# Gated linear attention and a mixture of experts on one core: output matmuls by term, column sums in mid-step, another bank for one tile, and a new step plan at the start

## The chip, the cores and the metric

The kernel runs on one core of one Trainium2 chip. The metric is the device time of one execution in microseconds (us). Engines are named as in the profile: PE is TensorE's matmul, PEld its weight load, DVE is VectorE, ACT is ScalarE, POOL is GpSimd, SP is SyncE, which issues the DMAs.

## The reference

Attention first: for each of 4 batches and 8 heads a state of 48 by 48 decays by a gate and takes an outer product at each of 768 positions. Its outputs are the tokens (3072 by 384) of a mixture of 8 experts, whose weights are balanced over tokens and experts in eight rounds.

```
f = 1 / (1 + exp(-f_logit))
for t in range(S):
    state = f[:, :, t, :, None] * state + einsum('bhd,bhe->bhde', k[:, :, t], v[:, :, t])
    y[:, :, t] = einsum('bhd,bhde->bhe', q[:, :, t], state)
x = y as (3072, 384)
P = exp(x @ w_gate - max)
for _ in range(8):
    P /= P.sum(1, keepdims=True) + 1e-09
    P /= P.sum(0, keepdims=True) + 1e-09
    P *= N / E
out = sum over e of P[:, e:e+1] * (relu(x @ w1[e]) @ w2[e])
```

## The kernel before

Every fp32 matrix is split into two fp16 halves, high and low (xh and xl, w1h and w1l, hh and hl and so on), and a product takes three matmuls: high by high, low by high, high by low. The high half is made by ACT, the low one by DVE, from the same source, so a low half follows its high half.

The work is in three stages.

**Lead stage (to some 390 us).** 24 items, each 128 positions of one batch and all heads, in two chunks of 64, run through a chain of steps: gates by ACT's sigmoid, decay products by DVE's scans (`r`, and the one written over `fl`, which the profile calls q), scaled keys `kb` in two halves, their transposes `kt`, scores `aps`, masked scores `am` and their halves `ah`, `al`, new states `kvps`, `st` and their halves `sh`, `sl`, and the outputs `yps`. From `yps` ACT makes xh and DVE xl, the tokens; the matmul `lps` gives the gate logits. Items 0, 1 and 2 use `early_item` (transposes on PE), the others `item` (transposes by DMA). Each `yield` in an item ends a step. A loop counts steps in `g`: in each it advances every live item by one step, then the weight loads that are due in this step (`loads[g]`, set with `at_steps`), and then takes work from a filler:

```
        for gen in loads.pop(g, []):
            next(gen, None)
        put_off[0] = g < 18
        fill([n for at_, n in FILL if g >= at_][-1])
```

The filler is the first two experts on the tokens that are ready, tile by tile (`moe_tile`: 128 tokens; two groups of 36 matmuls `hps` of 128 columns, then 24 matmuls `yps<-w2,h` of 384 columns) for the first three of eight groups of tokens, and `moe` (384 tokens) for the others. `fill(n)` issues n units; a unit is one matmul of 384 columns or three of 128. `FILL` gives the units per step: (12, 4.7) means 4.7 units a step from step 12 on. A filler tile ends with `yr`, an ACT copy, and a DMA to a scratch buffer; its `hl` (lines 382 and 431) is DVE's low half of the hidden layer, which may be put off and made up for (`settle`). Regular items start every 8 steps from step 22 (`LEADS`), and their DMAs four steps earlier.

All instructions are pinned: each engine takes them in the order in which the program issues them, so a step's place in the program is its place in each engine's queue. SP is a queue too: a DMA that waits for its buffer holds those behind it.

Expert 0's weights are `first[0..7]` (four pieces of w1, four of w2), expert 1's `second[0..7]`. Each is a generator of three steps: DMA; then the high half on ACT (line 346); then the low half on DVE (line 350). Their raw pieces share buffers, so the second expert's DMA of a piece waits for the first's conversion.

`warm(n)` issues n matmuls on constants, whose result is not used; the first item begins with `warm(20)` while its data are on the way.

**Middle stage (to 502 us).** `sinkhorn` balances the weights in steps (its column sums are a matmul `sk_c` with a matrix of ones, lines 127 to 136), beside the rest of the filler, `fill(LEAD)` with LEAD = 8 in each step, and beside `convert` and `prepare_w1`, which make sums and halves for the last stage. The last three pairs of the filler are `raws`.

PSUM tiles of the filler come from two pools of two banks each in turn (`bank`: an even count takes `psm`, an odd one `psn`). At the end of the stage `psn` and the items' banks are given up to the pool `pk`.

**Last stage (to the end).** Experts 2 to 7 by a scheme with 15 products in place of 18 (banks kb_A to kb_F), and their second layer `kyps`. The change does not touch it.

In `item`, the outputs are issued for each of four head pairs p and two chunks c, six matmuls each, the fifth of them the first that reads `sl`:

```
                pr = [(vhw, ah[:, n, :]), (vlw, ah[:, n, :]), (vhw, al[:, n, :])]
                if c >= c0:
                    pr += [(shw[:, w], qh[:, cs[n]]), (slw[:, w], qh[:, cs[n]]), (shw[:, w], ql[:, cs[n]])]
```

`early_item` already issues them term by term. Line 278 is the helper `mm`, through which all matmuls of this path go.

Of the kernel before, what the change touches and what calls it, by code (L numbers as in the profile page):

```python
# [12 lines left out]
ALU = mybir.AluOpType  # L13
# [5 lines left out]
NP = H // 2  # L19
C = 64  # L20
# [56 lines left out]
NB = NP * CT  # L77
TS = CT * C
LEADS = 22
FILL = ((0, 12), (1, 10), (2, 0), (5, 2), (6, 0), (7, 6), (11, 0), (12, 4.7), (22, 8.7), (43, 8.2))  # L80
LEAD = 8
EPRIO = 100
WPRIO = 150
# [18 lines left out]
def sinkhorn(nc, pool, psp, tag, identf, onesf, lg, pe, mm, pin, scale=1.0):  # L102
    sm = pool.tile([128, 2], F32, name="sk_sm")
    pin(nc.vector.tensor_reduce(out=sm[:, 0:1], in_=lg.rearrange("p a e -> p (a e)"), axis=AX.X, op=ALU.max))
    yield
    ps = psp.tile([128, 128], F32, name="sk_t", tag=tag)
    mm(transpose=True, out=ps[0:1, :], in_=sm[:, 0:1], identity=identf)
    row = pool.tile([1, 1], F32, name="sk_r")
    yield
    pin(nc.vector.tensor_reduce(out=row, in_=ps[0:1, :], axis=AX.X, op=ALU.max))  # L110
    yield
    ps = psp.tile([128, 1], F32, name="sk_m", tag=tag)
    mm(out=ps, lhsT=onesf[0:1, :], rhs=row, start=True, stop=True)
    yield
    pin(nc.vector.tensor_scalar(out=sm[:, 1:2], in0=ps, scalar1=-scale, scalar2=None, op0=ALU.mult))
    pin(nc.scalar.activation(out=pe, in_=lg, func=AF.Exp, bias=sm[:, 1:2], scale=scale))
    yield
    yield
    rs = pool.tile([128, NT], F32, name="sk_rs")
    cs = pool.tile([128, NE], F32, name="sk_cs")  # L120
    for it in range(8):
        pin(nc.vector.tensor_reduce(out=rs, in_=pe, axis=AX.X, op=ALU.add))
        pin(nc.vector.tensor_scalar(out=rs, in0=rs, scalar1=1e-9, scalar2=None, op0=ALU.add))
        pin(nc.vector.reciprocal(out=rs, in_=rs))
        yield
        pin(nc.vector.tensor_tensor(out=pe, in0=pe, in1=rs[:, :, None].to_broadcast([128, NT, NE]), op=ALU.mult))
        pin(nc.vector.tensor_reduce(out=cs, in_=pe.rearrange("p a e -> p e a"), axis=AX.X, op=ALU.add))
        yield
        ps = psp.tile([128, NE], F32, name=f"sk_c{it}", tag=tag)
        mm(out=ps, lhsT=onesf, rhs=cs, start=True, stop=True)  # L130
        yield
        pin(nc.vector.tensor_scalar(out=cs, in0=ps, scalar1=1e-9, scalar2=None, op0=ALU.add))
        pin(nc.vector.reciprocal(out=cs, in_=cs))
        pin(nc.vector.tensor_scalar(out=cs, in0=cs, scalar1=float(N / NE), scalar2=None, op0=ALU.mult))
        yield
        pin(nc.vector.tensor_tensor(out=pe, in0=pe, in1=cs[:, None, :].to_broadcast([128, NT, NE]), op=ALU.mult))
        yield
# [3 lines left out]
def general(ctx, tc, qkf, vt, wg, w1, w2, out):  # L141
# [63 lines left out]
    lg = gc.tile([128, NT, NE], F32, name="glg")  # L205
    pe = gc.tile([128, NT, NE], F32, name="gpe")
    nc.sync.dma_start(out=lg.rearrange("p (u t) e -> p u t e", t=TT), in_=lgd.rearrange("u p t e -> p u t e"))
    for _ in sinkhorn(nc, gc, gs, "ps", identf, onesf, lg, pe, lambda transpose=False, **kw: (nc.tensor.transpose if transpose else nc.tensor.matmul)(**kw), lambda ins: ins):
        pass
    nc.sync.dma_start(out=ped.rearrange("u p t e -> p u t e"), in_=pe.rearrange("p (u t) e -> p u t e", t=TT))  # L210

    with tc.For_i(0, U) as u:
# [37 lines left out]
def fast(ctx, tc, qkf, vbd, wg, w1, w2, out, flag):  # L250
# [18 lines left out]
    def pin(ins):  # L269
        engine = ins.ins.engine  # L270
        if fixed[0]:
            if engine in last:
                behind(ins, last[engine])
            last[engine] = ins
        return ins

    def mm(transpose=False, **kw):
        ins = (nc.tensor.transpose if transpose else nc.tensor.matmul)(**kw)  # L278
        if order:
            behind(ins, order[-1])  # L280
        order.append(ins)
# [52 lines left out]
    def load(e, k, j):  # L334
        src = (w1 if k == 1 else w2)[e, j]
        n = 4 * (k - 1) + j
        if n < 6:
            raw = xp.tile([128, 1152], F32, name=f"w{k}r_{e}_{j}", tag=f"x{'hl'[n % 2]}{3 - n // 2}", bufs=1)[:, 0:768]
        else:
            raw = rp.tile([128, 768], F32, name=f"w{k}r_{e}_{j}", tag="wraw")  # L340
        raw = raw.rearrange("p (a f) -> p a f", f=256 if k == 1 else DM)
        nc.sync.dma_start(out=raw, in_=src)
        yield
        wh, wl = ((wp1 if e else wp0).tile(list(raw.shape), F16, name=f"w{k}{q}_{e}_{j}", tag=f"w{q}") for q in "hl")
        scale = W1S if k == 1 else W2S
        pin(nc.scalar.activation(out=wh, in_=raw, func=AF.Copy, scale=scale))
        pair = [wh, None]
        ws[e][k - 1].append(pair)
        yield
        pin(nc.vector.scalar_tensor_tensor(out=wl, in0=raw, scalar=scale, in1=wh, op0=ALU.mult, op1=ALU.subtract))  # L350
        pair[1] = wl
# [140 lines left out]
    def warm(n):  # L492
        ps = bank([128, 512], f"wps{banks[0]}")
        for _ in range(n):
            mm(out=ps, lhsT=ind[:, 0:128], rhs=ind[:, 0:NB * C], start=True, stop=True)

    def settle(n=2):
        for low in owed[:n]:
            low()
        del owed[:n]  # L500

    def early_item(i):
# [59 lines left out]
            pin(nc.vector.tensor_tensor(out=carry[0, i + 1], in0=kv1[0:R], in1=st[:, 1], op=ALU.add))  # L562

        if not i:
            warm(20)
        transposed(0, 0)
        yield
        for rs, ks in heads:
# [37 lines left out]
        c0 = 0 if i else 1  # L606
        pin(nc.scalar.activation(out=sh[:, c0:], in_=st[:, c0:], func=AF.Copy, scale=SS))
        settle()
        if i:
            transposed(0, 1)  # L610
            transposed(1, 1)
        yield
        pin(nc.vector.tensor_tensor(out=al, in0=am, in1=ah, op=ALU.subtract))
        pin(nc.vector.scalar_tensor_tensor(out=sl[:, c0:], in0=st[:, c0:], scalar=SS, in1=sh[:, c0:], op0=ALU.mult, op1=ALU.subtract))
        yield
        if not i:
            xt[0] = xalloc(0)
# [35 lines left out]
    def item(i):  # L653
# [93 lines left out]
        xh, xl = xof(u)  # L747
        tok = slice(s % TT * TS, s % TT * TS + TS)
        yps = psa.tile([128, NP, TS], F32, name=f"yps_{i}", tag="y", bufs=1)
        for p in range(NP):  # L750
            for c in range(CT):
                n, w = CT * p + c, slice((c * NP + p) * 96, (c * NP + p) * 96 + 128)
                vhw, vlw = vhs[i % 3][:, w], vls[i % 3][:, w]
                pr = [(vhw, ah[:, n, :]), (vlw, ah[:, n, :]), (vhw, al[:, n, :])]
                if c >= c0:
                    pr += [(shw[:, w], qh[:, cs[n]]), (slw[:, w], qh[:, cs[n]]), (shw[:, w], ql[:, cs[n]])]
                for m, (a, x) in enumerate(pr):
                    mm(out=yps[:, p, c * C:(c + 1) * C], lhsT=a, rhs=x, start=(m == 0), stop=(m == len(pr) - 1))
        yield
        for si, so in PCS:  # L760
            pin(nc.scalar.activation(out=xh[so + (tok,)], in_=yps[si], func=AF.Copy, scale=YS * XS))
# [121 lines left out]
    def go(gen, n=1):  # L883
        for _ in range(n):
            next(gen, None)

    first = [load(0, 1 + n // 4, n % 4) for n in range(8)]
    second = [load(1, 1 + n // 4, n % 4) for n in range(8)]
    wgen = gate_weights()
# [25 lines left out]
    for n in range(2, 8):  # L915
        at_steps(first[n], *((0,), (5,), (0, 7), (0, 8), (3, 9), (5, 10))[n - 2])
    for n in range(8):
        at_steps(second[n], 4 + n, *((17, 20), (17, 20), (18, 21), (18, 21), (22, 25), (23, 26), (24, 27), (25, 28))[n])
    begin = {LEADS + STEPS * (i - 3): i for i in range(3, NT)}
    while live or g < max(begin):  # L920
        if g == 2:
            third = early_item(2)
            go(third)
        if g == 7:
            go(third)
        if g == 10:
            live.append(third)
        if g + 4 in begin:
            live.append(item(begin[g + 4]))
        for it in list(live):  # L930
            if next(it, it) is it:
                live.remove(it)
        for gen in loads.pop(g, []):
            next(gen, None)
        put_off[0] = g < 18
        fill([n for at_, n in FILL if g >= at_][-1])
        g += 1
    actx.close()
    xq = ctx.enter_context(tc.tile_pool(name="xq", bufs=1, reuse_waits="tile"))
# [100 lines left out]

    def raws():
        for e, u in RAW[-3:]:
            yield from moe(e, u, ws[e])
            done[0] += 1

# [8 lines left out]
    converts = [convert(b, left(b)) for b in range(B)]  # L1054
    work = [converts[0]]
    kw = None
    step = 0
    while True:
        more = fill(LEAD)
        if not more and kw is None:  # L1060
            wctx0.close()
            kw = ctx.enter_context(tc.tile_pool(name="kw", bufs=4, reuse_waits="tile"))
            filler = raws()
            more = fill(0)
        if not more:
            break
        next(chain, None)
        for gen in list(work):
            if next(gen, work) is work:
                work.remove(gen)  # L1070
        step += 1
        if step in (28, 50, 66):
            work.append(converts[{28: 1, 50: 2, 66: 3}[step]])
        if step == 46:
            work.append(chained(prepare_w1(ORDER[0][0], j) for j in range(2)))
    for _ in chain:
        pass
    for gen in work:
        if gen is not converts[3]:
            for _ in gen:  # L1080
# [223 lines left out]
```

## Time and profile before

| | |
|---|---|
| median of 3 runs | 1555.04 us (1554.15 to 1555.78) |
| the profiled execution | 1555.37 us, span 1553.6 us |
| granted clock of PE, mean | 0.997 |
| PE busy | 1522.1 us (98%), 13462 matmuls |
| DVE, ACT, POOL busy | 1097.2, 776.5, 514.5 us |

A row of a timeline has start (us from the span's start), time, engine, line, operation, what it writes and reads, size and count, and in brackets the idle time of the engine just before it and what ended it. Rows of busy time by stretch have the stretch, its length, then busy us of PE, PEld, DVE, ACT and POOL with instruction counts, then the granted PE clock, the share of the DMA engines and GB/s. A matmul's own time holds its latency; matmuls overlap, so their cost is the distance between starts.

### The profile page before, as it was taken

To read this page: it belongs to the slowest core of one execution; us is meant where nothing else is said; L and a number is where in the kernel's file an instruction comes from. 1 tells how busy PE (TensorE), PEld (TensorE's weight loads), DVE (VectorE), ACT (ScalarE), POOL (GpSimd) and SP (SyncE) were. 2 spreads that over 40 slices of the span, in tenths; PEclk is the share of its full clock that TensorE was granted. 3 is DMA by queue.
4 is the path that set the end of the run, shared out by engine and by line. 5 is a ranking of instruction groups with operands and counts; after the bars stand their busy time and mean duration, and the time that the engine had idled before them with its cause. 6 is when DMAs were issued, how large, how long until landed. Compare 5 with 4: busy or idle time off the path is not lost.

```text
span 1553.6 us, 32490 instructions
## 1 busy us (share of the span) xinstructions
PE 1522.1 (98%) x13462; PEld 1105.9 (71%) x13462; DVE 1097.2 (71%) x1810; ACT 776.5 (50%) x1489; POOL 514.5 (33%) x656
## 2 busy tenths in 40 slices
PE   7899999999999999999999999999999999999998
PEld 5688886666555777777777777777777777777775
DVE  8887888885775766676767776666766666665654
ACT  6655565553343655555455554545444444445432
POOL 1244444444519102333333322223222232222211
PEclk9999999999999999999999999999999999999999
DMA  9355554441002122232322231121112112000011
GB/s 267 102 137 132 127 140 120 119 116 31 26 22 63 55 72 79 63 89 67 92 67 82 77 87 62 41 62 51 62 47 66 44 38 57 22 20 12 6 57 65
DMA packets 89679, 114.39 MB, mean 74 GB/s; under 512 B 50641, under 2 KB 67153, under 8 KB 89521
## 3 DMA queue, kind: packets, MB, share of 16 engines
q1 hardware_dynamic: 89520, 112.22, 25.7%
q8 instruction: 107, 1.75, 0.5%
q14 instruction: 52, 0.42, 0.1%
HBM read 88.41 MB, written 14.16 MB: 66 GB/s over the span
## 4 chain that ended last, share of the span: by engine, by line
PE 90%; DVE 6%; ACT 1%; POOL 1%; issue 1%; ACTq 0%; DVEq 0%; POOLq 0%
PE kyps L278 36%; PE yps L278 12%; PE hps L278 9%; PE kb_A L278 8%; PE kb_B L278 8%; PE kb_D L278 6%; PE kb_C L278 4%; PE kb_E L278 2%; PE kb_F L278 2%; PE kvps L278 1%; PE aps L278 1%; POOL xs L962 1%; PE wps L278 1%; DVE hl L382 1%; DVE w2l L350 0%
## 5 line engine op out<-in xcount | busy, mean ns | idle before, releaser
L1119 POOL TENSOR_TENSOR acc<-acc,yt 128x384 f32<-128x384 f32 x172 | 173.3, 1007 | 629.8 <-ACT yt L1118 629.8
L278 PE MATMUL kyps<-k2l,kh 128*128 128x384 f16 x1152 | 375.5, 326 | 0.0
L278 PE MATMUL kyps<-k2h,kl 128*128 128x384 f16 x1152 | 375.5, 326 | 0.0
L278 PE MATMUL kyps<-k2h,kh 128*128 128x384 f16 x1152 | 375.5, 326 | 0.0
L278 PEld LDWEIGHTS <-k1h 128*128 128x128 f16 x2880 | 281.5, 98 | 70.4
L278 PEld LDWEIGHTS <-kh 128*128 128x128 f16 x2304 | 225.4, 98 | 103.9
L1118 ACT ACTIVATE yt<-kyps,pes 128x384 f32<-128x384 f32 x172 | 100.0, 581 | 323.1 <-PE kyps L278 321.2
L278 PEld LDWEIGHTS <-k1l 128*128 128x128 f16 x1440 | 140.6, 98 | 64.1 <-issue 7.1
L1115 DVE SCALAR_TENSOR_TENSOR acc<-kyps,pes,acc 128x384 f32<-128x384 f32 x92 | 56.9, 618 | 172.0 <-PE kyps L278 172.0
L278 PEld LDWEIGHTS <-kl 128*128 128x128 f16 x1152 | 112.7, 98 | 44.7
L1212 ACT ACTIVATE cp<-kb_A 128x512 f32<-128x512 f32 x144 | 86.2, 598 | 86.3 <-PE kb_A L278 85.8
L278 PE MATMUL yps<-w2h,hl 128*128 128x384 f16 x384 | 125.6, 327 | 3.5 <-DVE hl L431 3.5
L278 PE MATMUL yps<-w2l,hh 128*128 128x384 f16 x384 | 125.5, 327 | 1.8 <-DVE w2l L350 1.8
L278 PE MATMUL yps<-w2h,hh 128*128 128x384 f16 x384 | 125.5, 327 | 0.2 <-DVE hl L382 0.2
L278 PEld LDWEIGHTS <-w1h 128*128 128x128 f16 x1344 | 97.4, 98 | 35.4 <-issue 4.6
L1212 ACT ACTIVATE cp<-kb_B 128x512 f32<-128x512 f32 x144 | 87.1, 605 | 49.9 <-DVE kb_B L1214 49.8
L278 PEld LDWEIGHTS <-hh 128*128 128x128 f16 x768 | 74.6, 98 | 47.5 <-issue 2.8
L1217 DVE TENSOR_TENSOR cp<-kb_D,cp 128x512 f32<-128x512 f32 x144 | 98.8, 686 | 12.8 <-PE kb_D L278 11.8
L278 PE MATMUL hps<-xl,w1h 128*128 128x128 f16 (+1 forms) x672 | 84.9, 257 | 1.4 <-DVE xl L640 0.7
L278 PE MATMUL hps<-xh,w1h 128*128 128x128 f16 (+1 forms) x672 | 84.1, 257 | 1.7 <-ACT xh L637 1.1
L278 PE MATMUL hps<-xh,w1l 128*128 128x128 f16 (+1 forms) x672 | 84.4, 258 | 0.0
L278 PE MATMUL kb_A<-xbh,k1h 128*128 128x256 f16 x288 | 78.5, 273 | 0.8 <-ACT yr L399 0.6
(244 smaller groups left out, 3616.9 us busy)
## 6 DMA issues: line engine op xcount, KB each, us to landing
wm<-in_w_dram SPq DMA_DIRECT2D x64, 384.0 KB, 3.0
q<-in_qkf_dram SPq DMA_DIRECT2D x23, 672.0 KB, 5.2
vr<-in_vbd_dram SPq DMA_DIRECT2D x24, 384.0 KB, 3.5
ys<-yr SPq DMA_DIRECT2D x48, 192.0 KB, 2.4
k1r<-in_w_dram SPq DMA_DIRECT2D x24, 384.0 KB, 3.0
k2r<-in_w_dram SPq DMA_DIRECT2D x24, 384.0 KB, 3.0
yb<-ys SPq DMA_DIRECT2D x48, 192.0 KB, 2.3
out_dram<-acc SPq DMA_DIRECT2D x24, 192.0 KB, 1.9
```

Of the source, the lines that this page charges most:

```text
L278: ins = (nc.tensor.transpose if transpose else nc.tensor.matmul)(**kw)
L382: held[0] = pin(nc.vector.scalar_tensor_tensor(out=tl, in0=ps, scalar=0.0, in1=th, op0=ALU.max, op1=ALU.subtract))
L962: pin(nc.gpsimd.tensor_tensor(out=block(r), in0=block(p), in1=block(q), op=ALU.add if op == '+' else ALU.subtract))
L1115: pin(nc.vector.scalar_tensor_tensor(out=y, in0=ps, scalar=p, in1=y, op0=ALU.mult, op1=ALU.add))
L1118: pin(nc.scalar.activation(out=yt, in_=ps, func=AF.Copy, scale=p))
L1119: pin(nc.gpsimd.tensor_tensor(out=y, in0=y, in1=yt, op=ALU.add))
L1212: pin(nc.scalar.activation(out=fresh(ev[2]), in_=bk, func=AF.Copy))
L1217: pin(nc.vector.tensor_tensor(out=fresh(ev[4]), in0=bk, in1=old, op=ALU.add if ev[2] == '+' else ALU.subtract))
```

## The change

Six edits.

1. `warm(20)` before the first item's transposes becomes `warm(12)`.
2. In `early_item`, for items 1 and 2, the two transposes of the second chunk are issued one step later, behind `al` and `sl`. Item 2 takes its second and third step at steps 6 and 9 in place of 7 and 10, and all that follow one sooner; its DMAs stay at step 2. The units per step are cut anew: none at step 9, six at 10 and 11, 5.3 from 12, 8.7 from 21, 8.1 from 43. Low parts of the filler are put off until step 17, not 18.
3. The second expert's halves are made one to three steps sooner, its DMAs are issued where they were; from step 21 on the due loads stand behind the step's filler, not ahead of it.
4. In `item`, the outputs are issued term by term over all p and c, with the terms that read `sl` last.
5. In `sinkhorn` the column sum's matmul is handed to the loop, which issues it after 5 of the next 8 units.
6. Ahead of the last pair of the filler the bank count skips one where that puts the last tile into `psm`.

```
-FILL = ((0, 12), (1, 10), (2, 0), (5, 2), (6, 0), (7, 6), (11, 0), (12, 4.7), (22, 8.7), (43, 8.2))
+FILL = ((0, 12), (1, 10), (2, 0), (5, 2), (6, 0), (7, 6), (9, 0), (10, 6), (12, 5.3), (21, 8.7), (43, 8.1))
...
-        mm(out=ps, lhsT=onesf, rhs=cs, start=True, stop=True)
-        yield
+        yield lambda: mm(out=ps, lhsT=onesf, rhs=cs, start=True, stop=True)
...
-            warm(20)
+            warm(12)
...
         settle()
+        yield
+        pin(nc.vector.tensor_tensor(out=al, in0=am, in1=ah, op=ALU.subtract))
+        pin(nc.vector.scalar_tensor_tensor(out=sl[:, c0:], in0=st[:, c0:], scalar=SS, in1=sh[:, c0:], op0=ALU.mult, op1=ALU.subtract))
         if i:
             transposed(0, 1)
             transposed(1, 1)
-        yield
-        pin(nc.vector.tensor_tensor(out=al, in0=am, in1=ah, op=ALU.subtract))
-        pin(nc.vector.scalar_tensor_tensor(out=sl[:, c0:], in0=st[:, c0:], scalar=SS, in1=sh[:, c0:], op0=ALU.mult, op1=ALU.subtract))
         yield
...
+        m = 0
+        for a, x, own, lo in ((vhs[i % 3], ah, True, 0), (vls[i % 3], ah, True, 0), (vhs[i % 3], al, True, 0), (shw, qh, False, c0), (shw, ql, False, c0), (slw, qh, False, c0)):
+            for c in range(lo, CT):
+                for p in range(NP):
+                    n, w = CT * p + c, slice((c * NP + p) * 96, (c * NP + p) * 96 + 128)
+                    mm(out=yps[:, p, c * C:(c + 1) * C], lhsT=a[:, w], rhs=x[:, n, :] if own else x[:, cs[n]], start=(m == 0), stop=(a is slw or (c < c0 and x is al)), skip_group_check=True)
+                    m += 1
...
-        at_steps(second[n], 4 + n, *((17, 20), (17, 20), (18, 21), (18, 21), (22, 25), (23, 26), (24, 27), (25, 28))[n])
+        at_steps(second[n], 4 + n, *((16, 19), (16, 19), (17, 20), (17, 20), (20, 22), (21, 23), (22, 24), (23, 25))[n])
...
-        if g == 7:
+        if g == 6:
             go(third)
-        if g == 10:
+        if g == 9:
             live.append(third)
...
-        for gen in loads.pop(g, []):
-            next(gen, None)
-        put_off[0] = g < 18
+        if g < 21:
+            go_all(g)
+        put_off[0] = g < 17
         fill([n for at_, n in FILL if g >= at_][-1])
+        go_all(g)
...
         for e, u in RAW[-3:]:
+            if (e, u) == RAW[-1]:
+                banks[0] += (banks[0] + FT + TT) % 2 == 0
             yield from moe(e, u, ws[e])
...
-        more = fill(LEAD)
+        more = fill(LEAD * 5 / 8)
+        if held_mm:
+            held_mm()
+        more = fill(LEAD * 3 / 8)
...
-        next(chain, None)
+        held_mm = next(chain, None)
```

The fallback `general` and the loop that ends the middle stage call what `sinkhorn` hands them at once.

More of the change, by code (lines that the diff above doesn't have):

```diff
@@ L207, in general @@
     nc.sync.dma_start(out=lg.rearrange("p (u t) e -> p u t e", t=TT), in_=lgd.rearrange("u p t e -> p u t e"))
-    for _ in sinkhorn(nc, gc, gs, "ps", identf, onesf, lg, pe, lambda transpose=False, **kw: (nc.tensor.transpose if transpose else nc.tensor.matmul)(**kw), lambda ins: ins):
-        pass
+    for held in sinkhorn(nc, gc, gs, "ps", identf, onesf, lg, pe, lambda transpose=False, **kw: (nc.tensor.transpose if transpose else nc.tensor.matmul)(**kw), lambda ins: ins):
+        if held:
+            held()
     nc.sync.dma_start(out=ped.rearrange("u p t e -> p u t e"), in_=pe.rearrange("p (u t) e -> p u t e", t=TT))
@@ L749, in item @@
         yps = psa.tile([128, NP, TS], F32, name=f"yps_{i}", tag="y", bufs=1)
[L750 to L758, printed above, removed]
+        m = 0
[5 more added lines that the diff above has]
+                    m += 1
         yield
@@ L885, in go, with go_all @@
             next(gen, None)
+    def go_all(g):
+        for gen in loads.pop(g, []):
+            next(gen, None)
     first = [load(0, 1 + n // 4, n % 4) for n in range(8)]
@@ L1056, in fast @@
     kw = None
-    step = 0
+    step, held_mm = 0, None
     while True:
-        more = fill(LEAD)
+        more = fill(LEAD * 5 / 8)
+        if held_mm:
+            held_mm()
+        more = fill(LEAD * 3 / 8)
         if not more and kw is None:
@@ L1075, in fast @@
             work.append(chained(prepare_w1(ORDER[0][0], j) for j in range(2)))
-    for _ in chain:
-        pass
+    while True:
+        if held_mm:
+            held_mm()
+        held_mm = next(chain, 0)
+        if held_mm == 0:
+            break
     for gen in work:
```

## The prediction

> **What bounds the kernel now.** I read the page first, then the busy time by stage, then what TensorE waits for, then the timelines of the stages with waits in them.
>
> ```profile
> span 1553.6 us, 32490 instructions
> PE 1522.1 (98%) x13462; PEld 1105.9 (71%) x13462; DVE 1097.2 (71%) x1810; ACT 776.5 (50%) x1489; POOL 514.5 (33%) x656
> ```
> ```profile
> 0.00:80.00 80.00, 65.42 (x801) 47.11 (x802) 68.93 (x119) 49.08 (x90) 16.43 (x26) 0.96 0.67 186
> 80.00:380.00 300.00, 296.36 (x4147) 226.89 (x4144) 246.13 (x405) 164.52 (x338) 131.77 (x119) 1.00 0.47 117
> 380.00:502.50 122.50, 119.93 (x741) 71.34 (x739) 83.76 (x158) 46.39 (x95) 73.21 (x101) 1.00 0.10 35
> 502.50:1553.00 1050.50, 1040.43 (x7781) 760.60 (x7780) 698.35 (x1129) 516.52 (x967) 293.07 (x413) 1.00 0.19 57
> ```
>
> The columns of the second fence are stretch, length, then busy time of PE, PE's weight load, DVE, ACT and POOL. From 80 us on TensorE is the bound, and nothing in the change shortens its own work there but a spacing. So a gain is either idle time of TensorE or constant (warming) matmuls. Idle is 14.6 us before 80, 3.6 in 80 to 380, 2.6 in 380 to 502.5; the 10 us behind 502.5 belong, but for kb_A's first wait, to code that the change leaves as it is. The ceiling is therefore about 21 us plus the warming matmuls, and the first 80 us hold most of it. There DVE is busy 68.9 of 80 us. What ends the waits:
>
> ```profile
> PE yps L278 <- DVE hl L431: 3.5, 2, 2.5
> PE yps L278 <- DVE sl L742: 2.7, 3, 1.2
> PE sk_c L278 <- DVE sk_cs L127: 1.9, 3, 1.3
> PE hps L278 <- ACT xh L637: 1.1, 1, 1.1
> PE ktp L278 <- DVE hl L431: 0.9, 1, 0.9
> PE kb_A L278 <- ACT yr L399: 0.6, 1, 0.6
> ```
>
> The three numbers are us in total, times, longest. Each part of the change points at a row of this list.
>
> **Part 1: 12 constant matmuls in place of 20 at first.**
>
> ```profile
> L278 PE MATMUL wps<-ind 112*128 112x512 f16 x13 | 5.7, 632 | 3.0 <-DVE ind L306 3.0
> ```
> ```profile
> 2.98 7.39 PE L278 MATMUL wps<-ind 112*128 112x512 f16 x20 [2.98 <-DVE ind L306]
> ...
> 12.11 0.22 PE L278 MATMUL aps<-qh,kb 112*128 112x64 f16 x2
> ```
> ```profile
> 6.82 1.28 ACT L531 ACTIVATE kb<-q 48x512 f16<-48x512 f32 x2 [2.30 <-DVE q L528]
> ```
> ```profile
> 8.51 1.39 DVE L569 TENSOR_TENSOR kb<-q,kb 48x512 f16<-48x512 f32 x2
> 9.93 0.69 DVE L573 TENSOR_TENSOR ql<-q,qh 112x512 f16<-112x512 f32 x1
> ```
>
> The first row is the group between 3.2 and 8.4 us: 13 matmuls in 5.7 us, about 0.43 each (they overlap at the ends). Twelve from 2.98 end near 8.1. kb's high half is there at 6.82+1.28 = 8.10, so the first transposes start near 8.15, where now the twenty hold TensorE to about 10.2. Behind them are five constant matmuls, the low transposes (kb's low half ends at 9.90), two more constants, and `aps`, which needs `ql` (10.62). Now `aps` starts at 12.11; without the excess ql is the last to come, so about 10.65. That is 1.4 us for the whole chain of the first tile, and through the first tile for DVE, which works without a pause from there on. Ends: if the clock opens earlier in another execution, the twenty are cheaper and the gain is 0; it cannot be over 10.2 - 8.1 = 2.1. I take 1.4, since this execution's rows give it.
>
> The clock is what the eight might have bought. These rows show it, full from 8.9 to 25.9, half after a stretch with idle TensorE:
>
> ```profile
> 8.90:25.90 17.00, 14.51 (x196) 10.25 (x194) 14.09 (x24) 13.86 (x26) 0.21 (x1) 1.00 1.04 286
> 26.00:32.70 6.70, 5.92 (x54) 4.45 (x55) 6.60 (x11) 4.58 (x10) 1.41 (x1) 0.50 1.03 268
> ```
>
> With twelve, TensorE still has the transposes and the five constants behind them, so it is busy from 2.98 past 10 without a gap of any size. The Trainium skill, TensorE: Matmul & The Clock Gate, Part 1 (the HAM clock gate), says that the clock opens after one busy window of about 3.4 us that runs free of the program, so that the number of cold matmuls differs from run to run. By that rule the twelve are enough, yet twenty may cost less than here, and the part's gain would be 0 to 1.4. The 17.0 us of full clock fit five such windows, so this trace agrees; its run-to-run spread no trace here shows.
>
> **Part 2: item 2 a step sooner, filler moved from step 9 to step 11, transposes of items 1 and 2 a step later.**
>
> ```profile
> 36.17 0.32 PE L278 MATMUL yps<-w2l,hh 128*128 128x384 f16 x1 [1.20 <-DVE w2l L350]
> ...
> 36.82 0.40 PE L278 MATMUL yps<-ah,vh 128*128 128x64 f16 x8
> ...
> 38.22 0.28 PE L278 MATMUL kvps<-vh,kt 128*112 128x96 f16 x2
> ...
> 47.14 0.37 PE L278 MATMUL ktp<-identh,kb 112*128 112x112 f16 x4 [0.74 <-DVE kb L569]
> ```
> ```profile
> 20.00:40.00 20.00, 15.74 (x196) 11.75 (x195) 19.18 (x29) 11.01 (x20) 2.06 (x4) 0.83 0.98 255
> ```
> ```profile
> 40.46 0.49 ACT L452 ACTIVATE yr<-yps 128x384 f32<-128x384 f32 x1 [6.34 <-PE yps L278]
> 40.85 1.34 ACT L637 ACTIVATE xh<-yps 96x384 f16<-96x384 f32 x4
> ```
> ```profile
> 39.05 0.56 DVE L562 TENSOR_TENSOR carry<-kvps,st 112x384 f32<-112x384 f32 x1 [0.52 <-PE kvps L278]
> ...
> 42.22 1.49 DVE L640 SCALAR_TENSOR_TENSOR xl<-yps,xh 96x384 f16<-96x384 f32 x4 [2.01 <-ACT xh L637]
> ...
> 45.69 1.39 DVE L569 TENSOR_TENSOR kb<-q,kb 48x512 f16<-48x512 f32 x2
> ```
>
> Item 1's outputs end at 38.22, but xh runs at 40.85, behind `yr`, which waits for a filler tile. DVE, busy 19.2 of the 20 us up to 40, then stands idle 0.52 + 2.01 = 2.53 us. With step 9 empty of filler the outputs go ahead of the six filler matmuls with the 1.20 us wait, and with filler in step 11 `yr` is issued after xh. DVE also has item 2's scan, now at step 12, to fill the hole. So kb's low half of item 2, at 47.08 now, comes 2.5 us sooner on top of part 1. Up to it two steps of 5.3 units of filler are done where three of 4.7 were: 3.5 units fewer, 0.16 us each (four of them lie between 36.17 and 36.82), 0.6 us of work still owed. Net 1.9. Ends: 0, if something else holds DVE there, and 2.5 + 1.2.
>
> The transposes a step later: the second of them waits 0.93 us for hl to free its bank (the 0.9 row above). A step later hl is done; its copy is needed by kv1 only after 48 output matmuls (1.4 us). Gain 0.9; ends 0 and 0.93. Item 2's DMAs are issued at the same step as before, and that low parts are put off one step less (17 for 18) goes with item 2's earlier end.
>
> **Part 3: the second expert's weights sooner, from step 21 behind the filler.**
>
> ```profile
> 74.64 0.34 PE L278 MATMUL yps<-w2h,hl 128*128 128x384 f16 x1 [2.54 <-DVE hl L431]
> ```
> ```profile
> 65.68 1.67 DVE L350 SCALAR_TENSOR_TENSOR w2l<-w2r,w2h 128x768 f16<-128x768 f32 x1
> ...
> 69.10 3.41 DVE L350 SCALAR_TENSOR_TENSOR w2l<-w2r,w2h 128x768 f16<-128x768 f32 x2
> ...
> 73.91 1.28 DVE L431 SCALAR_TENSOR_TENSOR hl<-hps,hh 128x512 f16<-128x512 f32 x2
> ```
> ```profile
> 66.49 3.71 POOL L691 TENSOR_TENSOR kb<-q,kb 48x512 f16<-48x512 f32 x2
> ```
>
> Four w2l conversions stand in the DVE queue ahead of the hl that TensorE wants at 72.1. The change moves them three steps up, two ahead of it by far. But two of them (steps 24 and 25) then sit right behind item 3's scan, where POOL starts on item 3. Beside POOL's kb a w2l takes 1.67, and two take 3.41. Counted at 1.7 each, w2l, w2l and item 3's vl, three instructions with two inputs in memory, end some 5 us behind the scan, and hl is again 2 to 2.5 us late, as TensorE comes there sooner. I take 0; ends 2.5 (no slowing) and -1.0.
>
> The rule is in the Trainium skill, SBUF — State Buffer, Who interferes with whom: a VectorE instruction with two SBUF inputs contends with a GpSimd instruction that reads SBUF. By it the moved conversions are slow again and the sum keeps 0 here; a sum without contention would have 2.5 us more. The trace agrees: 1.67 us beside kb.
>
> **Part 4: outputs of items 3 to 23 term by term.**
>
> ```profile
> 331.48 0.20 PE L278 MATMUL yps<-qh,sl 112*128 112x64 f16 x1 [1.05 <-DVE sl L742]
> ...
> 332.80 0.33 PE L278 MATMUL yps<-w2h,hl 128*128 128x384 f16 x1
> ```
> ```profile
> 330.08 1.33 DVE L742 SCALAR_TENSOR_TENSOR sl<-st,sh 112x768 f16<-112x768 f32 x1
> 331.34 0.55 DVE L382 SCALAR_TENSOR_TENSOR hl<-hps,hh 128x384 f16<-128x384 f32 x1
> ```
>
> sl is needed at the fifth matmul now, at the forty-first then, some 1.2 us later, so the waits of 2.7 us in all vanish. Not all is kept: hl follows sl on DVE and is ready at 331.9, and the filler behind the outputs, at 332.8 now, would come near 331.6. I take 2.1 of 2.7; ends 0.8 and 2.7. The number of matmuls is the same. 44 take 1.32 us here (30.0 ns); the 48 of item 1, already by term, 1.40 (29.2 ns). 0.8 ns by 48 by 21 items is 0.8; I take 0.5, ends 0 and 0.8.
>
> **Part 5: column sums of the balancing in mid-step.** Five units, 0.8 us, now lie between the step's start and the matmul. The waits of 1.9 us are three, the longest 1.3: it keeps 0.5, the others go. Gain 1.4. What waits for the matmul on DVE waits longer:
>
> ```profile
> 449.14 0.17 DVE L132 TENSOR_SCALAR sk_cs<-sk_c 128x8 f32<-128x8 f32 x1 [2.60 <-PE sk_c L278]
> ```
>
> There DVE is ahead of TensorE and can lose 0.8 more; queued behind it are hl and conversions, which TensorE does not wait for then. Ends 1.9 and -0.8.
>
> **Part 6: the last tile in the other pool.** kb_A no longer waits for the last yr: 0.6 (ends 0 and 0.6). The bank that is used a turn sooner was emptied microseconds before.
>
> **Sum.** 1.4 + 1.9 + 0.9 + 0 + 2.1 + 0.5 + 1.4 + 0.6 = 8.8 us. The profiled execution took 1555.37 us (span 1553.6), so 1546.6; the median of the runs is 0.3 lower, so 1546.2.
>
> **Rivals.**
> A: only the late parts come through (4 to 6, 4.6 us), with 1 us at most of parts 1 and 2, since DVE's backlog before 75 us takes the rest. For: DVE is busy 68.9 of 80 us. Against: the 2.53 us of idle DVE have a nameable cause that goes. Time 1549.5 to 1551.
> B: no change. Each wait comes back at the next item, because DVE is busy 246 of 300 us and the steps are cut anew (5.3, 8.7 and 8.1 units). For: the second wait for hl L431 (3.5 - 2.5 = 1.0 us, at 158) is not addressed. Against: 18% slack. Time 1552 to 1557.
> C, slower: the clock. If the shorter burst does not open it at 8.9 us, the 14.5 us of work up to 25.9 take up to twice as long. The idle time of TensorE in that stretch, 2.5 us, can take some and the late parts give 4.6 back: 14.5 - 2.5 - 4.6 = +7, 1562. It decides once the clock opens two windows (6.8 us) late or more. Against: no gap in TensorE's work up to 10 us.
> D: hl at 72 us goes as well, and all else holds: 1543 to 1544.
>
> **How the numbers follow.** A measurement of this kernel tells 0.2%, 3.1 us. Forecast 0.57 (own range 1544 to 1549), A 0.20, D 0.08, B 0.10, C 0.05. Faster: forecast, A, D = 0.85; same: most of B, 0.09; slower: C and a tail of B, 0.06. Range 1542.5 to 1551: it leaves out B and C and a little of each tail.
>
> **What would show it.** Right: `aps` near 10.7 us; xh of item 1 ahead of yr and no wait of 1.1 for it; no row yps <- sl over 0.3; sk_c waits near 0.5; kb_A without yr; hl still 2 us late near 70. Wrong: the granted clock at a half before 20 us; DVE without any pause from 13 to 75 us yet item 2's outputs no sooner than 4 us; new rows of yps or ktp waiting for hl between 80 and 380.

## The result: 9.7 us faster, and the profile after

The changed kernel takes 1544.86 us (median of 6 runs, 1544.19 to 1545.37) against 1554.55 us (6 runs, 1553.77 to 1555.78): a ratio of 0.9937, interval 0.9924 to 0.995. The forecast was 1546.2. The profiled execution took 1544.66 us, span 1542.9. The two lines of the page, then busy time by stretch, with the columns as before:

```profile
span 1542.9 us, 32479 instructions
PE 1518.7 (98%) x13454; PEld 1104.3 (72%) x13454; DVE 1091.6 (71%) x1810; ACT 775.2 (50%) x1489; POOL 517.0 (34%) x656
```
```profile
0.00:80.00 80.00, 68.61 (x886) 50.47 (x887) 68.19 (x120) 50.12 (x92) 20.14 (x27) 0.96 0.66 189
80.00:380.00 300.00, 298.78 (x4103) 226.17 (x4101) 246.28 (x409) 165.86 (x341) 139.65 (x129) 1.00 0.48 117
380.00:502.50 122.50, 120.12 (x765) 74.64 (x764) 84.29 (x162) 51.86 (x105) 65.46 (x90) 1.00 0.13 44
```

TensorE is idle 11.4 us before 80 (14.6 before the change), 1.2 in 80 to 380 (3.6). The third stretch can't be compared so, since the middle stage now ends inside it: kb_A begins at 492.57 us, where it began at 503.11. From kb_A to the end both kernels take 1050.3 to 1050.5 us, so the whole difference, 10.5 us in these two executions, arises before it.

What TensorE waits for now, the rows that answer to those of before:

```profile
PE yps L278 <- DVE hl L431: 3.0, 5, 1.4
PE hps L278 <- DVE hl L382: 1.5, 3, 1.0
PE ktp L278 <- ACT kb L531: 1.3, 1, 1.3
PE yps L278 <- DVE w2l L350: 1.0, 2, 0.5
PE kvps L278 <- DVE vl L583: 0.8, 1, 0.8
PE yps L278 <- ACT hh L428: 0.2, 1, 0.2
```

Four rows are gone: the waits for `sl`, for xh of item 1, for the column sums and, at kb_A, for `yr`; and ktp no longer waits for hl. The row of hl at L382, 1.5 us, is larger than it was (0.56), and the prediction's sum has no term for it. The first tile and item 2, on TensorE:

```profile
2.98 5.30 PE L278 MATMUL wps<-ind 112*128 112x512 f16 x12 [2.98 <-DVE ind L306]
8.24 0.53 PE L278 MATMUL ktp<-identh,kb 112*128 112x112 f16 x4
...
10.60 0.22 PE L278 MATMUL aps<-qh,kb 112*128 112x64 f16 x2
```

The first `aps` starts at 10.60 us (12.11 before). Item 1's and item 2's gain is seen on ACT and DVE:

```profile
38.16 1.34 ACT L637 ACTIVATE xh<-yps 96x384 f16<-96x384 f32 x4
39.81 0.49 ACT L452 ACTIVATE yr<-yps 128x384 f32<-128x384 f32 x1 [0.31 <-PE yps L278]
```
```profile
39.54 1.49 DVE L640 SCALAR_TENSOR_TENSOR xl<-yps,xh 96x384 f16<-96x384 f32 x4 [0.31 <-ACT xh L637]
41.88 1.38 DVE L569 TENSOR_TENSOR kb<-q,kb 48x512 f16<-48x512 f32 x2
```

xh now runs ahead of `yr`; DVE's idle time ahead of xl went from 2.01 to 0.31 us and the 0.52 ahead of `carry` is gone. kb's low half of item 2 ends at 43.26 us where it ended at 47.08: 3.8 us sooner, of which 1.5 is the start of `aps` and 2.3 this part.

### The profile page after: what moved, and what is told of

Same layout as the page of the kernel before. It is cut to its first block, busy times and chain, and to the rows that moved or that the text cites. A ratio compares the mean times of both kernels' runs of the same rounds, so it can differ in the third digit from the quotient of the medians.

```text
span 1542.9 us, 32479 instructions
## 1 busy us (share of the span) xinstructions
PE 1518.7 (98%) x13454; PEld 1104.3 (72%) x13454; DVE 1091.6 (71%) x1810; ACT 775.2 (50%) x1489; POOL 517.0 (34%) x656
## 3 DMA queue, kind: packets, MB, share of 16 engines
q8 instruction: 107, 1.75, 0.5%
## 4 chain that ended last, share of the span: by engine, by line
PE 91%; DVE 5%; ACT 2%; POOL 1%; issue 1%; DVEq 0%; ACTq 0%; POOLq 0%
PE kyps L278 36%; PE yps L278 12%; PE hps L278 9%; PE kb_A L278 8%; PE kb_B L278 8%; PE kb_D L278 6%; PE kb_C L278 4%; PE kb_E L278 2%; PE kb_F L278 2%; PE kvps L278 1%; PE aps L278 1%; POOL xs L965 1%; PE wps L278 0%; DVE w2l L350 0%; POOL k1s L1012 0%
## 5 line engine op out<-in xcount | busy, mean ns | idle before, releaser
L1229 DVE TENSOR_TENSOR cp<-kb_D,cp 128x512 f32<-128x512 f32 x144 | 98.7, 685 | 12.8 <-PE kb_D L278 11.8
```

The lines of the kernel that those rows point to most:

```text
L1229: pin(nc.vector.tensor_tensor(out=fresh(ev[4]), in0=bk, in1=old, op=ALU.add if ev[2] == '+' else ALU.subtract))
```

## The experiments

A part "alone" is the kernel before with only that edit; the other runs undo an edit or change a size in the changed kernel. (The kernels of parts 1 to 6 alone also issue the eight units of a middle step as five and three. This changes nothing that shows: in part 1 alone the stretch from the last gate to kb_A is as long as in the kernel before, to 0.02 us.) All ratios are against the kernel before, run on the same chip beside it (its medians there: 1554.84 for parts 1, 2, 4 and 5 alone, 1554.91 for part 3 alone, the 20 constants and the late conversion, 1555.21 for the rest).

**Part 1 alone.**

```
-            warm(20)
+            warm(12)
```

> The kernel before with 12 constant matmuls in place of 20 and nothing else changed. If the twenty only held TensorE past 8.1 us and DVE works without a pause behind the first tile, the whole chain up to 38 us comes 1.4 us sooner and stays so: 1553.2 against 1554.6, first scores near 10.6. Rival one: the backlog of DVE or the landing of item 1's data at 17.8 us takes it back, and the time is 1554.6 again although the first scores come sooner. Rival two: the clock opens later, TensorE's work up to 26 us runs at half clock, and the time is 1556 or more.

Measured 1554.14 us, 0.9999 (0.999 to 1.0008): 0.7 us by the medians, which the interval can't tell from nothing; the 1.4 that was expected did not come. In its trace `aps` starts at 10.60 us, as in the changed kernel, and kb_A 1.48 us sooner than in the profile of before. Why an execution's profile gives 1.5 and the times give half is shown by the opposite edit.

**The changed kernel with 20 constants**, everything else as changed.

```
-            warm(12)
+            warm(20)
```

> The changed kernel with 20 constant matmuls again. If the first tile's delay runs through DVE's chain, the time is 0.3 to 1.5 us above the changed kernel's, by where the clock opens (6.5 to 8.9 us in the traces so far): 1545.6, first scores at 10.9 to 12.1. Rival: in the changed kernel something else sets the pace behind the first tile, and the time is 1544.8 as with 12.

Measured 1545.0 us, 0.9939 (0.9925 to 0.9952), 0.1 us from the changed kernel, less than the 0.3 to 1.5 that was expected. Its TensorE rows:

```profile
2.98 6.27 PE L278 MATMUL wps<-ind 112*128 112x512 f16 x20 [2.98 <-DVE ind L306]
10.99 0.22 PE L278 MATMUL aps<-qh,kb 112*128 112x64 f16 x2
```

The twenty took 7.39 us in the profile of before and take 6.27 here: the same matmuls from the same start. Busy time between 6.7 and 8.3 us (first fence the kernel before, second this one) shows where:

```profile
6.70:8.30 1.60, 1.60 (x5) 0.60 (x4) 1.57 (x3) 1.26 (x2) 0.00 (x0) 1.00 0.96 366
```
```profile
6.70:8.30 1.60, 1.60 (x9) 0.77 (x8) 1.57 (x3) 1.26 (x2) 0.00 (x0) 1.00 0.99 372
```

Five matmuls run in the stretch before, nine here. The clock column says 1.00 in both, so it is the matmuls' rate that tells when the clock opens: before about 6.6 us here, near 8.9 there (the column does not show this first opening). Over the executions profiled with 20 constants `aps` began at 10.93, 10.99, 11.17, 11.25, 11.85, 12.11 and 12.14 us; with 12 it began at 10.60 to 10.71. So part 1 is worth 0.3 to 1.5 us by the phase of one execution, and 1.4 was nearly the dearest case. The Trainium skill, TensorE: Matmul & The Clock Gate, Part 1 (the HAM clock gate), says that the window is free-running and that the number of cold matmuls varies from run to run. The traces agree with that. The section puts the variation at ±500 ns; here the rate changed between 6.6 and 8.9 us in the seven executions with 20 constants, a spread of over 2 us, and the measurement decides.

**Four constants in the changed kernel.**

```
-            warm(12)
+            warm(4)
```

> The changed kernel with 4 constant matmuls in place of 12. If twelve are there to open the clock, four leave TensorE idle from 4.7 to 8.1 us, the clock opens only at 11.6 to 15, the scores and outputs of the first tile run at half clock, the first xh comes 2 to 3 us later, and the time is 1547 to 1548. Rival: the clock has no part in it, since DVE's chain and the landings set the pace, and the time is 1544.9 or a little less.

Measured 1546.46 us, 0.9943 (0.993 to 0.9957), 1.6 us more than the changed kernel's median and a little under the 1547 to 1548 that was expected. (The ratios of the two differ by 0.9 us only and their intervals overlap; the traces say 2 us.)

```profile
2.98 1.89 PE L278 MATMUL wps<-ind 112*128 112x512 f16 x4 [2.98 <-DVE ind L306]
8.25 0.53 PE L278 MATMUL ktp<-identh,kb 112*128 112x112 f16 x4 [3.39 <-ACT kb L531]
8.58 2.34 PE L278 MATMUL wps<-ind 112*128 112x512 f16 x5
...
11.94 0.31 PE L278 MATMUL aps<-qh,kb 112*128 112x64 f16 x2
```

After 3.39 us of idle TensorE the five constants take 2.34 us where the changed kernel's took 1.43, the pairs of `aps` take 0.29 to 0.31 us in place of 0.22 until the rate changes near 13.7 us, `aps` starts 1.34 later and kb_A 2.06. So rival C's mechanism exists, but its price with four constants is 2 us, not the +7 of the rival: only the five constants, `aps` and what follows it up to 13.7 us run at half the rate. Twelve bridge the gap up to kb's high half, four do not.

**Part 2 alone** (item 2's steps, the cut of the units, the transposes).

```
-        if g == 7:
+        if g == 6:
...
-        if g == 10:
+        if g == 9:
...
-        put_off[0] = g < 18
+        put_off[0] = g < 17
...
```

The lines of `FILL` and of the transposes, as under the change, belong to it too.

> The kernel before with the new step plan for item 2, its filler and the later transposes, and nothing else changed. If idle DVE (2.5 us between 38 and 42 us) and the bank wait of 0.9 us are what goes, 2.8 us: 1551.8, item 2's scores 2.5 us sooner, xh of item 1 ahead of yr. Rival: the second expert's conversions, still at their old steps, now stand in a shorter stretch, hl is later by what was won (wait of 4 to 5 us near 70 us in place of 2.5) and the time stays at 1554 to 1554.6; then the plan pays only together with part 3.

Measured 1552.24 us, 0.9985 (0.9976 to 0.9994): 2.6 us. The first `aps` of item 2 starts at 43.84 us where it started at 47.34. Of these 3.5 us 1.2 are the clock's phase, since this execution's very first `aps` stands at 10.93 and not at 12.11; 2.3 are the part's. The rival's longer wait near 70 us did not come (2.2 us). The list of waits shows what the shift of all steps gives and takes further on:

```profile
PE yps L279 <- DVE hl L432: 3.8, 5, 2.2
...
PE hps L279 <- DVE hl L383: 1.5, 3, 1.0
PE yps L279 <- DVE sl L743: 1.5, 3, 0.8
```

1.2 us of the waits for `sl` go by the shift alone, and the wait of 1.5 at hl L382 (L383 here) comes with it.

**Part 3 undone in the changed kernel**, and **part 3 alone**.

```
-        at_steps(second[n], 4 + n, *((16, 19), (16, 19), (17, 20), (17, 20), (20, 22), (21, 23), (22, 24), (23, 25))[n])
+        at_steps(second[n], 4 + n, *((17, 20), (17, 20), (18, 21), (18, 21), (22, 25), (23, 26), (24, 27), (25, 28))[n])
```

In the first of the two the due loads go back ahead of the filler as well; the second is the reverse of it, in the kernel before.

> The changed kernel with the second expert's weights back at their old steps and the due loads ahead of the filler in every step; all else as changed. In the changed kernel hl is late by 1.4 us at 68.7. If part 3 is worth next to nothing, as forecast, because the moved conversions are slowed beside POOL, the wait is 1.5 to 2.5 and the time 1545 to 1546 against 1544.9. Rival: with the old steps four conversions stand ahead of hl on a shorter lead, the wait grows to 4 us or more, and the time is 1547.5: then part 3 is needed for part 2.

Measured 1544.68 us, 0.9935 (0.9921 to 0.9948): undone, it costs nothing that can be measured.

> The kernel before with the second expert's weights sooner and the due loads behind the filler from step 21, nothing else changed. Undoing this part in the changed kernel cost 0.3 us. If it is worth as little by itself, because POOL slows the moved conversions, the wait of 2.5 us for hl near 72 us stays over 1.5 and the time is 1554 to 1554.8 against 1554.9. Rival: without part 2 TensorE comes to hl later, three conversions end in time, the wait goes and the time is 1552.4; then parts 2 and 3 take the same microseconds, and the single gains add up to more than the whole.

Measured 1554.11 us, 0.9993 (0.9984 to 1.0002). The hl that TensorE wants near 70 us waits 2.21 us with part 3 undone and 1.38 + 0.21 with it. The waits for hl with part 3 undone, then with part 3 alone:

```profile
PE yps L278 <- DVE hl L431: 3.4, 4, 2.2
```
```profile
PE yps L279 <- DVE hl L432: 2.8, 3, 1.0
PE ktp L279 <- DVE hl L432: 1.5, 1, 1.5
```

Alone, the wait of 2.5 gives way to two of 0.9, and the wait at ktp grows from 0.9 to 1.5: together 4.3 us, where the kernel before has 4.4. The time came as expected, the single wait of over 1.5 near 72 us did not. What makes hl late is in the rows of DVE and POOL in the changed kernel:

```profile
64.73 0.93 DVE L350 SCALAR_TENSOR_TENSOR w2l<-w2r,w2h 128x768 f16<-128x768 f32 x1
65.58 2.02 DVE L350 SCALAR_TENSOR_TENSOR w2l<-w2r,w2h 128x768 f16<-128x768 f32 x1
67.53 1.90 DVE L692 SCALAR_TENSOR_TENSOR vl<-vr,vh 128x768 f16<-128x768 f32 x1
69.36 0.68 DVE L431 SCALAR_TENSOR_TENSOR hl<-hps,hh 128x512 f16<-128x512 f32 x1
```
```profile
64.89 1.90 POOL L682 TENSOR_TENSOR q<-q 112x512 f32<-112x512 f32 x1 [3.42 <-DVE q L679]
66.75 3.70 POOL L691 TENSOR_TENSOR kb<-q,kb 48x512 f16<-48x512 f32 x2
```

Two w2l and vl end 4.7 us behind 64.73, beside POOL's q and kb: the collision that the prediction named (it said some 5). The first w2l starts ahead of POOL's q and takes 0.93 us; the second and vl, beside POOL, take 2.02 and 1.90.

**The low halves one step earlier still**, out of POOL's way.

```
-... (20, 22), (21, 23), (22, 24), (23, 25))[n])
+... (19, 21), (20, 21), (21, 22), (22, 23))[n])
```

> The changed kernel with the second expert's four w2 low halves at steps 21, 21, 22, 23 in place of 22 to 25 (their high halves at 19, 20, 21, 22). Two of them go into the 2.1 us in which DVE waits for hh at 56 us, and none stands beside item 3's work on POOL. If contention with POOL made hl late, a w2l takes 0.95 again in place of 1.4, the wait of 1.4 us for hl at 68.7 ends, and the time is 1543.4 to 1543.8. Rival: the wait has another cause (vl, or the order behind it) and stays over 1 us; the time is 1544.9.

Measured 1543.92 us, 0.9927 (0.9913 to 0.994), 0.1 above what was expected: the wait fell from 1.4 to 0.39 us and did not quite end. On the same chip beside it part 3 undone had taken 1544.68; the slowest of these five runs (1544.13) is just under the fastest of those five (1544.17).

```profile
56.41 1.83 DVE L350 SCALAR_TENSOR_TENSOR w2l<-w2r,w2h 128x768 f16<-128x768 f32 x2
...
64.78 0.94 DVE L692 SCALAR_TENSOR_TENSOR vl<-vr,vh 128x768 f16<-128x768 f32 x1
...
68.40 0.69 DVE L431 SCALAR_TENSOR_TENSOR hl<-hps,hh 128x512 f16<-128x512 f32 x1 [2.69 <-ACT hh L428]
```
```profile
66.88 0.63 ACT L689 ACTIVATE qh<-q 112x512 f16<-112x512 f32 x1 [1.77 <-POOL q L682]
```

Two w2l take 1.83 us together at 56.41 against 2.87 at 64.73, vl 0.94 against 1.90, and POOL's two kb 2.39 against 3.70. DVE is now done 2.7 us before hh lets it go on; what is left of the wait (0.39) is hh, which stands on ACT behind qh, which waits for POOL. kb_A starts 0.9 us sooner. The run moves the conversions as well as freeing them from POOL, so it doesn't separate the two. By the rows the slowing alone is enough: at 0.94 each, two w2l and vl from 64.73 on would end near 67.5, before the 68.40 at which hl could start here. So contention as the cause of part 3's zero is borne out by the rows, and no run shows it by itself.

**Part 4 alone** (outputs term by term).

```
-        for p in range(NP):
-            for c in range(CT):
...
+        for a, x, own, lo in ((vhs[i % 3], ah, True, 0), ... (slw, qh, False, c0)):
+            for c in range(lo, CT):
+                for p in range(NP):
```

> The kernel before with the outputs of items 3 to 23 term by term and nothing else changed. If the waits for sl end (2.7 us) and the closer spacing holds (29.2 in place of 29.8 ns, 48 matmuls, 21 items: 0.6 us), and hl behind sl gives some back, 2.6 us: 1552.0, no wait for sl over 0.3. Rival: DVE is late by the same amount at the next hl, the wait for sl is replaced by waits for hl of the same sum, and only the spacing is left: 1554.0.

Measured 1551.44 us, 0.998 (0.9971 to 0.9989): 3.4 us, the largest part. One wait for `sl` is left, 0.18 us. The place of the prediction's own rows, on TensorE and on DVE:

```profile
330.27 0.41 PE L279 MATMUL yps<-qh,sl 112*128 112x64 f16 x8
330.52 0.33 PE L279 MATMUL yps<-w2h,hl 128*128 128x384 f16 x1
330.68 0.32 PE L279 MATMUL yps<-w2l,hh 128*128 128x384 f16 x1
```
```profile
328.88 1.34 DVE L743 SCALAR_TENSOR_TENSOR sl<-st,sh 112x768 f16<-112x768 f32 x1
...
330.14 0.55 DVE L383 SCALAR_TENSOR_TENSOR hl<-hps,hh 128x384 f16<-128x384 f32 x1
```

The filler's matmul at 330.52 follows the outputs without a wait although the hl behind `sl` ends only at 330.69: it reads an earlier hl. The waits for hl are those of before (2.55 us at 74, 0.98 at 159), so nothing is given back, and the spacing inside the outputs falls from 29.8 to 29.2 ns: 0.6 by 48 by 21 items, 0.6 us.

The list of waits understates what they cost. From the first output matmul to the first matmul behind the outputs, the three items with a wait take 1.99, 2.65 and 2.83 us in the kernel before, the others 1.43. That is 0.56, 1.22 and 1.40 more for listed waits of 0.39, 1.05 and 1.23: 0.16 to 0.17 us more each, because the idle time is counted from the end of the matmul before, and without a wait the next one starts 0.16 us ahead of that end (0.03 us behind its start, where it takes 0.19). With part 4 alone the three take 1.40, 1.58 and 1.75: `sl` still costs 0.18 at 330.27, which the list doesn't show (`sl` ends at 330.22), and 0.35 at 358.47, of which it shows 0.18. Over the 21 items the outputs take 28.90 us in place of 32.11: 3.2 of the 3.4 us.

**Part 5 alone** (column sums in mid-step).

```
-        mm(out=ps, lhsT=onesf, rhs=cs, start=True, stop=True)
-        yield
+        yield lambda: mm(out=ps, lhsT=onesf, rhs=cs, start=True, stop=True)
```

> The kernel before with the column sums' matmul in mid-step and nothing else changed. If TensorE's three waits for the sums (1.9 us) shrink to 0.5 and nothing else moves, 1.4 us: 1553.2. The stretch from the last gate to the first kb_A shrank by 1.8 us with parts 5 and 6 together in the changed kernel beyond what is explained, so up to 2.3 (1552.3) is possible if each of the eight sums costs TensorE something besides the listed waits. Rival: DVE waits longer for the matmul, hl behind it is later, and the time is 1554.6 or 0.8 above.

Measured 1553.15 us, 0.9988 (0.9979 to 0.9997): 1.7 us. The stretch from the last gate to kb_A goes from 119.02 to 116.65 us, 2.37 less, where the listed waits only fell from 1.95 to 0.47 (1.48). The sums on TensorE, the kernel before and then this one:

```profile
399.74 0.39 PE L278 MATMUL sk_c<-sk_cs,onesf 128*128 128x8 f32 x2 [0.32 <-DVE sk_cs L127]
...
406.48 0.28 PE L278 MATMUL sk_c<-sk_cs,onesf 128*128 128x8 f32 x2
...
413.62 0.39 PE L278 MATMUL sk_c<-sk_cs,onesf 128*128 128x8 f32 x2 [0.34 <-DVE sk_cs L127]
...
420.48 0.39 PE L278 MATMUL sk_c<-sk_cs,onesf 128*128 128x8 f32 x2
...
442.07 0.39 PE L278 MATMUL sk_c<-sk_cs,onesf 128*128 128x8 f32 x2 [1.28 <-DVE sk_cs L127]
...
448.81 0.28 PE L278 MATMUL sk_c<-sk_cs,onesf 128*128 128x8 f32 x2
```
```profile
399.24 0.28 PE L278 MATMUL sk_c<-sk_cs,onesf 128*128 128x8 f32 x2
...
405.87 0.28 PE L278 MATMUL sk_c<-sk_cs,onesf 128*128 128x8 f32 x2
...
439.69 0.39 PE L278 MATMUL sk_c<-sk_cs,onesf 128*128 128x8 f32 x2 [0.47 <-DVE sk_cs L127]
...
446.43 0.28 PE L278 MATMUL sk_c<-sk_cs,onesf 128*128 128x8 f32 x2
```

A sum that comes late takes 0.39 us for its two passes, one in time 0.28, and 420.48 took 0.39 with no listed wait at all. Five of eight were late before, one is now. Sums in time follow each other at 6.63 to 6.64 us; from first to last sum the kernel before took 49.07 (399.74 to 448.81) and this one 47.19. The list of idle time leaves a part out. The second pass starts 0.132 us behind the first in a late sum, 0.028 in one in time. So the 2.37 us are 1.48 less of listed idle time, 0.16 more for each of two listed waits that are gone (as with `sl`), 0.10 for each of four sums that are no longer late, and 0.14 in two waits too short to be listed. The distances are measured; why the second pass comes later was not tried.

**Part 6 alone** (the last tile's pool).

```
+            if (e, u) == RAW[-1]:
+                banks[0] += (banks[0] + FT + TT) % 2 == 0
```

> The kernel before with the last tile of the filler in the other pool and nothing else changed. kb_A's first matmul no longer waits 0.63 us for the last yr: 1554.2 against 1554.8, within what can be told, and in the trace no wait at kb_A for yr. Rival: the tile that takes its bank a turn sooner waits for hl in place of it, and the stretch from the last gate to the first kb_A stays at 119.0 us.

Measured 1554.33 us, 0.9996 (0.9987 to 1.0005): 0.9 us by the medians, inside the interval. In its list of waits kb_A no longer waits for `yr` (0.63 before), and the stretch from the last gate to kb_A is 0.80 us shorter, 0.16 more than the listed wait again.

**The fourth batch's conversion three steps later**, on top of the earlier low halves. It tests where the new 1.5 us at hl L382 comes from.

```
-        if step in (28, 50, 66):
-            work.append(converts[{28: 1, 50: 2, 66: 3}[step]])
+        if step in (28, 50, 69):
+            work.append(converts[{28: 1, 50: 2, 69: 3}[step]])
```

> As early21 (w2 low halves at steps 21, 21, 22, 23), and the fourth batch's conversion begins at step 69 of the middle stage in place of 66. At 472 to 475 us TensorE waits 1.4 us for hl, with this conversion's first sums and the third batch's last halves ahead of it on DVE. If it is their meeting that makes hl late, the waits end and the time is 1 us below early21's: 1542.9 against 1554.9 before. Rival: the conversion comes too late for the last stage, or the waits only move: 1543.9 or more.

Measured 1543.11 us, 0.9925 (0.9911 to 0.9939), the lowest median of all: 11.8 us below the kernel before beside it, 1.75 below the changed kernel's median, though the two intervals of the ratio overlap.

```profile
PE hps L278 <- DVE hl L382: 0.6, 1, 0.6
PE yps L278 <- ACT hh L381: 0.6, 1, 0.6
```

The wait fell from 1.5 to 0.6, and 0.6 appears at hh on ACT; kb_A starts at 491.30 us against 491.70 without this edit. So by these two traces the conversion's place has a part in the wait (its sums stand ahead of the filler's hl on DVE), and 0.4 us can be had this way.

## Why the prediction came out, step by step

The forecast's way of going is the one that happened, and rivals A, B and C did not: both early and late parts came through. Its sum was 8.8, the time fell 9.7. That the two are so close is in part luck: parts 4 and 5 brought more than forecast, waits for hl at two places that no term stands for took about as much away, and part 1 is not worth its 1.4 by the times. Against equal amounts of filler done, the two profiles and the single runs give:

| step | predicted | found in the traces |
|---|---|---|
| parts 1 and 2, up to item 3 | 1.4 + 1.9 + 0.9 = 4.2 | 4.6 |
| part 3 | 0 (-1.0 to 2.5) | 0.35 of the above |
| part 4 | 2.1 + 0.5 = 2.6 | 3.4 |
| part 5 | 1.4 | 2.4 |
| part 6 | 0.6 | 0.8 |
| hl L431 between 158 and 196 | 0 | -0.6 |
| hl L382 near 475 | not there | -1.1 |

That is 9.5 (for part 4 the time of the run alone, for parts 5 and 6 its trace, for the others the two traces; the rows of hl are their listed idle time and 0.16 for each wait more). kb_A starts 10.5 us sooner, and the other 1.0 I can't place.

- **Part 1 was mis-sized.** The step took the rows of one execution in which the clock opened late. It named the other end (0) and the reason, yet chose the dear one. The two profiles do differ by 1.5 at `aps`; by the times the part is 0.1 to 0.7, which can't be told from nothing.
- **Part 2 was right in mechanism and size**: 2.3 at kb's low half of item 2, forecast 2.5 before the 0.6 of filler owed; by the times of the part alone 2.6, forecast 1.9 + 0.9. The transposes no longer wait for hl.
- **Part 3 was right to be put at zero, as far as can be told (0.35 in the traces, -0.2 and 0.8 in the times), and the collision that was its reason is there.** The remaining wait was 1.6 (1.38 + 0.21), not 2 to 2.5. Rival D, hl gone as well, did not come, but the earlier low halves show that it can.
- **Part 4: the step that failed is "hl follows sl".** It held that the next filler matmul needs the hl queued behind `sl`. The row at 330.52 shows that it does not. So the part came in near its upper end: 3.4 by the times, 3.2 in the outputs, where the three waits cost 3.2 and not the listed 2.7, and 0.5 of it stays.
- **Part 5 was mis-sized**, since it counted only the listed idle time. The late sums also cost their own 0.1 each, 0.16 more per wait than listed, and waits too short to be listed: 2.4 in the trace in place of 1.4. By the times it is 1.7, with an interval (0.5 to 3.3 us) that holds both.
- **Part 6 was right** in the wait that goes; the times (0.9) can't tell it from nothing.
- **A sign that was named as wrong came in part.** Waits of yps for hl begin at 170.66, 184.20 and 195.65 us (0.22, 0.23, 0.77) in place of one of 0.98 at 158. Together their idle time is 0.2 more, and they are three for one.
- **Not foreseen:** the 1.5 at hl L382. It comes with part 2, as the run of part 2 alone shows, and shrinks when the fourth batch's conversion is put later. Why it is longer than before is not shown: in the kernel before the same sums and halves stand between two hl (483.67 to 486.61 us), and TensorE waits 0.39 there. The prediction counted what the shift moves up to 80 us and not what it moves at 475.

The single parts add up to 0.7 + 2.6 + 0.8 + 3.4 + 1.7 + 0.9 = 10.1 us by the medians, the whole is 9.7. Each has an interval of some 1.4 us to either side, so they are additive as far as this can tell. They are not quite independent: 1.2 us of the waits for `sl` would have gone by part 2 alone.

## What to carry to other kernels

When a wait is removed, look up which copy of the operand the next instruction reads before charging a give-back: the queue order of the producer alone does not say that anyone waits. A wait's row in the list was a lower bound of what it cost, here by 0.16 us each; compare the distance of the same instructions in a period with the wait and in one without. What the clock's opening costs is not to be taken from one profile: take it from several, or from both ends.

## What the runs showed of the hardware

From the same start (2.98 us) and with the same 20 constants the clock opened so differently that `aps` began anywhere from 10.93 to 12.14 us. The profiled execution of before has nearly the latest opening, so a part of the 10.5 us by which kb_A moved between the two profiles is this phase. That the 9.7 between the medians holds less of it is likely, and not shown.

DVE and POOL slow each other both ways: w2l from 0.95 to 2.02 us, vl from 0.94 to 1.90, POOL's kb from 1.16 to 1.76 and 1.87. An instruction that began ahead of the other engine's kept its time: w2l 0.93 at 64.73, and vl 0.94 at 64.78 in the run with earlier low halves, each some 0.16 us before POOL's q, which took 1.90 both times, against 1.27 in the kernel before. The Trainium skill, SBUF — State Buffer, Who interferes with whom, has the pair (a VectorE instruction with two SBUF inputs, a GpSimd instruction that reads SBUF); the runs agree and give the price: 1.5 to 2.1 times the duration. With the same conversions in stretches in which POOL stands idle but for 0.2 us the time was 0.9 us below the changed kernel's median (0.76 below part 3 undone beside it); beside POOL they were worth nothing that the times can tell.
